# Attention with a routed feed-forward on one core: flag and index loads, part of the early second layer, the gate of the weight loads and the fill of the plain arms moved

## The chip, the core and the metric

The kernel runs on one core of a Trainium2 chip. A core has TensorE (PE in the profile; its weight loads are the row PEld), VectorE (DVE), ScalarE (ACT), GpSimd (POOL) and SyncE (SP), each with an instruction stream of its own; they meet through semaphores, and data moves through 16 DMA engines. The metric is the device time of one execution in microseconds.

## The reference, cut to what matters

Chunked attention (4 batches, 8 heads, 768 positions of 64 numbers) gives 3072 tokens of 512 numbers. Each token then goes through the one expert out of eight that scores highest for it.

```python
for c in range(nc):                                    # chunks of 32 queries
    k_full = np.concatenate([mem_k, k_ctx], axis=2)    # 8 memory keys, 16 left, own 32, 8 right
    scores = scale * np.matmul(q_c, k_full.transpose(0, 1, 3, 2))
    a = softmax(scores)
    out[:, :, c_start:c_end] = np.matmul(a, v_full)
x = out.transpose(0, 2, 1, 3).reshape(B * S, H * D)
logits = x @ w_gate                                    # [3072, 8]
expert_idx = np.argmax(logits, axis=1)
for e in range(E):                                     # the tokens of expert e
    h = np.maximum(x_sorted[lo:hi] @ w1[e], 0.0)       # 512 -> 1024
    y_sorted[lo:hi] = h @ w2[e]                        # 1024 -> 512
y = gate_w[:, None] * y_sorted[inv_perm]
```

How many tokens an expert gets is known only at run time. Everything is float32, and a float32 matmul shows as two records of PE and two of PEld.

## The kernel before, in words

**Attention stage (to about 140 us of the span).** 32 blocks of 96 tokens go through transposes, scores, exponentials and values. Behind them run the logits, the routing and a scatter of each block's rows to `x_dram`, ordered by expert (`scatter_one`, on POOL). The scatters wait in the list `spread`, and `scatter_some` issues them; each is made to follow the last PE instruction that was issued before it (`behind`).

**Early rows.** The first 256 rows of expert 0 are computed while the routing of the last blocks is still under way. `early_ops` is a list of closures: one transposition, eight pieces of the first layer (`first`), then the second layer of the first 128 rows in four parts (`part_of`). Each part holds 4 float32 matmuls of 256 columns; the second and the fourth end with `early_out`, an ACT operation that writes half of the row block `y00`.

**End of the stage.** `count_up` is a chain of some forty small DVE operations that makes the tables of the experts' stage: `cases` (which arm each expert takes, and a flag that says whether it is a plain one), `bases` (first rows), `rows`, `good`. Then engines read such values into registers: PE reads the arm's number of every expert (`load_index`, L1228), DVE and ACT read six flags each (`plain_on`, L1243), and all read `good` (L1244). Between them PE does the last early parts. `nc.tensor.addr_align(PAGE, 0, 0)` makes PE go on at the start of a page of 256 instructions.

**Barrier.** `tc.tile_critical` (L1821, L1899) opens the experts' stage. All engines wait there for what was issued before. SP waits for the last scatter to land and for ACT's last operation (L1821) and then lets the others go (L1899).

**Experts' stage.** Its plan is written out by hand: `op` notes an instruction with the semaphore counts that it needs, `emit` issues it. On PE each expert has an interlude and a `Switch`, a jump table with one arm for each width and form:

* An interlude transposes the results of the expert before (`turn_y`, L538). That of expert 0 instead does the second layer of the early rows 128 to 255 (tile `sum_z`, 8 float32 matmuls of 512 columns).
* A **split** arm multiplies the two halves of the tokens by a seven-product scheme: 14 products for the first layer, 7 for the second, 448 LDWEIGHTS and MATMUL instructions in all.
* A **plain** arm, for experts 1 to 6 with at most 240 tokens, multiplies directly (`plain`). Four `pair` calls make the first layer (banks P, Q, Z, P) and two the second. The last bank is filled in two column halves (`groups=2`), which gives twice as many matmuls of half the width: 80 float32 matmuls, 320 instructions, so the arm reaches into a second page.
* Near its end an arm issues a hint for the arm of the next expert (L1813); the branch out of the arm and the jump of the next `Switch` have line L1829.

In this execution expert 1 (200 tokens wide, from 211.4 us) and expert 6 (168, from 420.3 us) take plain arms. The others take split ones.

**Counts in a plain arm.** Other engines wait for PE's and ACT's running counts, and both forms of an arm must end on the same ones. A split arm adds 21 to PE's count, one for each product. A plain arm sets the counts by `upto`: in `before` the four pairs of the first layer bring PE to 1, 2, 3 and 14 of 21, the rest to 15, 16, 17, 18 and 21. ACT's seven outputs bring its count to 1 to 6 and then, with the last one, to the end.

**SP's queue.** For each expert SP issues, in this order, the rows of the next one (`load_x`, 8 DMAs, L1417), w1 of the one after it (`get_w(e + 2, 0)`, 4 DMAs of 512 KB, L1490) and its w2 (`get_w(e + 2, 1)`, one DMA of 2 MB, L1489). The weights of expert e + 2 replace those of e, so each load waits until PE and DVE have read the old ones.

On DVE and ACT an `If` on the flag of the expert chooses between the instructions of the two forms (L1845).

Of the kernel before, what the change touches and what calls it, by code (L numbers as in the profile page):

```python
# [82 lines left out]
PAGE = 256  # L83
LB = 16
# [442 lines left out]
def ordinary(ctx, tc, q, k, v, mem_k, mem_v, moe_w_gate, moe_w1, moe_w2, out, good):  # L527

    nc = tc.nc
# [542 lines left out]
    def early_rows():  # L1072

        x0T = e0pool.tile([128, DM // 128, NER], F32, name="x0T")
        def turn_early():
            nc.vector.transpose(
                x0T.rearrange("p k (b j) -> p k b j", j=32), x0.rearrange("p b (k i) -> p k b i", k=4)
            )

        def first(f):  # L1080
            ph = ps_s.tile([128, 2, 512], F32, tag="s", name="ph0")[:, 0, 0:NER]
            for c in range(DM // 128):
                mm(
                    ph,
                    lhsT=ms[0]["w1"][:, c, 128 * f : 128 * f + 128],
                    rhs=x0T[:, c],
                    start=c == 0,
                    stop=c == DM // 128 - 1,
                )
            nc.scalar.activation(h0[:, f], ph, AF.Relu)  # L1090

        hold = {}

        def part_of(part):
            half, f = part // 2, F // 256 * (part % 2)
            if part % 2 == 0:
                hold["y"] = ps_s.tile([128, 2, 512], F32, tag="s", name="py0")
            py, sl = hold["y"][:, 0, 0 : DM // 2], slice(DM // 2 * half, DM // 2 * half + DM // 2)
            second_layer(py, 0, range(f, f + F // 256), sl)
            if part % 2 == 1:  # L1100
                early_out(0, py, sl)

        early_ops.append(turn_early)
        for f in range(F // 128):
            early_ops.append(lambda f=f: first(f))
        for part in range(4):
            early_ops.append(lambda part=part: part_of(part))
# [5 lines left out]
    with tc.manual_schedule():  # L1113
# [112 lines left out]
        def load_index(*of):  # L1226
            for e in of:
                index.append(nc.tensor.value_load(cases[0:1, e : e + 1], min_val=0, max_val=len(arms_of(e)) - 1))  # L1228

        while spread:  # L1230
            if len(early_ops) == 3:
                load_index(0, 1, 2)
            do_early(1)
            scatter_some(1)
# [3 lines left out]
        assert len(index) == 3 and len(early_ops) == 2  # L1238
        plain_on = {}
        for name, eng in (("DVE", nc.vector), ("ACT", nc.scalar)):  # L1240
            for e in range(E):
                if can_be_plain(e):
                    plain_on[name, e] = eng.value_load(cases[0:1, E + e : E + e + 1], min_val=0, max_val=1)  # L1243
# [3 lines left out]
        load_index(3, 4)  # L1247
        do_early(1)
        load_index(5, 6, 7)
# [36 lines left out]
    def op(eng, fn, reads=(), writes=(), dma=None, where="after", pace=False, by=16, upto=None):  # L1286
# [6 lines left out]

        if pace:
            after(("PE", counts["PE"]))
# [187 lines left out]
    def get_w(e, which):  # L1483
# [8 lines left out]
        op("SP", fn, [], [(name, e % 2, q) for q in ("21", "rest")], dma=f"{name}{e % 2}", by=(64, 16)[which])  # L1492
# [145 lines left out]

    def interlude(e):

        before = ("before", e)
        if e == 0:
# [8 lines left out]
            for i in range(3):  # L1651
                sums1[0][0][i]()
            for part in range(4):
                op("PE", lambda n, part=part: second_layer(Z[:, 0], 1, [2 * part, 2 * part + 1]), [], ["z0"], where=before)
# [13 lines left out]
    def plain(e, ends):  # L1668
# [36 lines left out]
        mid = start["PE"] + 14  # L1705
        for j, (bank, names) in enumerate((sums_p, sums_q, sums_z, sums_p)):
# [7 lines left out]
                mid if j == 3 else start["PE"] + j + 1,  # L1714
# [8 lines left out]
        for m, (bank, names) in enumerate((sums_q, sums_p)):  # L1723
# [7 lines left out]
            if m == 0:  # L1731
                first = [("h", a, b, 0) for a in range(2) for b in range(2) if a * b == 0]
                pair(*second, w2n + first, mid + 1, of=range(C2 - 2))
                pair(*second, [("h", 1, 1, 0)], mid + 2, of=range(C2 - 2, C2))
# [11 lines left out]
    def expert(e):  # L1746
# [14 lines left out]
        def usual():  # L1761
# [10 lines left out]
            assert not sends  # L1772
            if e < E - 1:
                get_x(e + 1)
                tick()
# [26 lines left out]
    for g in range(2):  # L1802
        sends.append(lambda pace, g=g: op("POOL", one_op(lambda: put(early["y", g], lab0[:, g, 0:1])), [("yb", NY - 1)] if g else [], [], dma=f"early{g}", pace=True))
# [17 lines left out]
    with tc.tile_critical(no_gpsimd_drain=True):  # L1821
# [14 lines left out]
        for name in ("POOL", "SP", "ACT", "DVE"):  # L1836
            eng, done = engines[name], set()
            for s in (s for s in plan if s[0] == name):
                if s[4] == "after":
                    emit(s)  # L1840
                elif s[4][1] not in done:
                    e = s[4][1]
                    done.add(e)
                    if (name, e) in plain_on:
                        with eng.If(plain_on[name, e]):  # L1845
                            for x in steps(name, ("plain", e)):
                                emit(x)
# [56 lines left out]
```

## Time and profile before

| what | us |
|---|---|
| runs of this kernel, median of 3 (lowest, highest) | 503.57 (502.87, 503.97) |
| the profiled execution | 503.97 |
| its span, first to last instruction | 502.2 |
| PE busy | 472.9 |
| PEld busy | 440.1 |
| DVE busy | 282.0 |
| ACT busy | 207.4 |
| POOL busy | 145.9 |

The profiled execution is the slowest of the three runs. Its span leaves out 1.8 us around the first and the last instruction. PE is the engine that is busy nearly all the time, so the places to look at are those where it stands still or runs slowly. In a timeline, the bracket behind an instruction is the idle time of its engine before it, and what ended it; "issue" means that the engine waited for nothing that the profile shows, its sequencer for example.

### The profile page before, as it was taken

To read this page: it belongs to the slowest core of one execution; us is meant where nothing else is said; L and a number is where in the kernel's file an instruction comes from. 1 tells how busy PE (TensorE), PEld (TensorE's weight loads), DVE (VectorE), ACT (ScalarE), POOL (GpSimd) and SP (SyncE) were. 2 spreads that over 40 slices of the span, in tenths; PEclk is the share of its full clock that TensorE was granted. 3 is DMA by queue.
4 is the path that set the end of the run, shared out by engine and by line. 5 is a ranking of instruction groups with operands and counts; after the bars stand their busy time and mean duration, and the time that the engine had idled before them with its cause. 6 is when DMAs were issued, how large, how long until landed. Compare 5 with 4: busy or idle time off the path is not lost. (4 is left out here: it accounts for less than half of the span.)

```text
span 502.2 us, 9216 instructions
## 1 busy us (share of the span) xinstructions
PE 472.9 (94%) x3320; PEld 440.1 (88%) x3320; DVE 282.0 (56%) x548; ACT 207.4 (41%) x388; POOL 145.9 (29%) x191
## 2 busy tenths in 40 slices
PE   4999999999999699997799999999999999999993
PEld 3899999999997479997799999987778999989992
DVE  4466587667556178922446666655346776445511
ACT  3676666566621046311253155243313643144312
POOL 3000223313434127334034134313230550352003
PEclk9999999999999899999699999999999999999997
DMA  9999998899898289789805294583432986500002
GB/s 220 182 208 208 228 263 228 223 217 280 232 233 263 71 253 196 189 249 209 239 31 123 50 281 128 109 230 105 99 72 65 301 171 194 136 6 27 1 0 87
DMA packets 103059, 82.99 MB, mean 165 GB/s; under 512 B 40309, under 2 KB 85966, under 8 KB 102992
## 3 DMA queue, kind: packets, MB, share of 16 engines
q1 hardware_dynamic: 94576, 67.94, 57.6%
q0 software_dynamic: 6912, 13.54, 8.1%
q8 instruction: 45, 0.74, 0.7%
q10 hardware_dynamic: 1504, 0.59, 0.5%
q14 instruction: 22, 0.18, 0.1%
HBM read 65.62 MB, written 21.28 MB: 173 GB/s over the span
## 5 line engine op out<-in xcount | busy, mean ns | idle before, releaser
L1452 POOL DMA_INDIRECT out_dram<-y,lab x42 | 48.7, 1159 | 155.4 <-ACT y L1439 30.9
L934 POOL DMA_INDIRECT lab<-x_dram,rows x42 | 52.8, 1258 | 53.1 <-PE sum_r L533 19.8
L533 PE MATMUL sum_p<-xsT,w 128*128 128x144 f32 (+7 forms) x256 | 50.8, 345 | 4.9 <-issue 3.8
L533 PE MATMUL o<-v,ex 128*96 128x65 f32 x512 | 52.8, 246 | 0.0
L533 PEld LDWEIGHTS o<-v,ex 128*96 128x96 f32 x512 | 50.4, 165 | 1.4 <-issue 1.3
L533 PEld LDWEIGHTS sum_p<-xsT,w 128*128 128x128 f32 x256 | 42.8, 194 | 9.7 <-issue 5.7
L533 PE MATMUL sum_p<-h,w 128*128 128x144 f32 (+9 forms) x320 | 50.4, 314 | 0.0
L533 PE MATMUL sc<-qT,kT 128*128 128x192 f32 x256 | 49.2, 336 | 0.0
L533 PEld LDWEIGHTS sum_p<-h,w 128*128 128x128 f32 x320 | 46.3, 191 | 2.4
L847 POOL DMA_INDIRECT x_dram<-xr,dest x32 | 29.6, 926 | 54.9 <-PE o L533 36.0
L704 ACT ACTIVATE ex<-sc,cst 128x256 f32<-128x256 f32 x96 | 38.5, 471 | 13.8 <-PE sc L533 11.6
L1388 ACT COPY sum_r<-sum_p 128x640 f32<-128x640 f32 x36 | 24.4, 677 | 46.0 <-PE sum_p L533 45.7
L533 PEld LDWEIGHTS sc<-qT,kT 128*128 128x128 f32 x256 | 42.0, 195 | 0.0
L655 ACT COPY qT<-tqk 64x384 f32<-64x384 f32 x60 | 30.0, 500 | 28.6 <-PE tqk L538 27.8
L673 DVE COPY kT<-tqk 64x384 f32<-64x384 f32 x58 | 32.0, 552 | 11.0 <-PE tqk L538 10.2
L533 PE MATMUL sum_q<-t,s 128*128 128x144 f32 (+5 forms) x192 | 38.2, 348 | 0.0
L533 PE MATMUL sum_r<-t,w 128*128 128x144 f32 (+5 forms) x192 | 37.0, 340 | 0.0
L533 PE MATMUL sum_p<-t,s 128*128 128x144 f32 (+5 forms) x192 | 37.0, 341 | 0.0
L533 PEld LDWEIGHTS sum_q<-t,s 128*128 128x128 f32 x192 | 33.2, 196 | 2.5
L533 PEld LDWEIGHTS sum_p<-t,s 128*128 128x128 f32 x192 | 32.2, 191 | 2.4
L1406 DVE STREAM_TRANSPOSE xsT<-xs 128x1280 f32<-128x1280 f32 (+1 forms) x16 | 22.4, 1427 | 20.6 <-DMA xs<-x_dram 11.3
L533 PEld LDWEIGHTS sum_r<-t,w 128*128 128x128 f32 x192 | 31.8, 190 | 2.3
(183 smaller groups left out, 774.8 us busy)
## 6 DMA issues: line engine op xcount, KB each, us to landing
w<-in_moe_w_dram SPq DMA_DIRECT2D x36, 512.0 KB
w<-in_moe_w_dram SPq DMA_DIRECT2D x7, 2048.0 KB, 11.5
xs<-x_dram SPq DMA_DIRECT2D x56, 160.0 KB
kn<-in_k_dram SPq DMA_DIRECT2D x16, 384.0 KB
qn<-in_q_dram SPq DMA_DIRECT2D x16, 384.0 KB
x_dram<-zeros SPq DMA_DIRECT2D x8, 396.0 KB
v<-in_v_dram SPq DMA_DIRECT2D x24, 128.0 KB
v<-in_v_dram SPq DMA_DIRECT2D x24, 112.0 KB
```

Of the source, the lines that this page charges most:

```text
L533: i = nc.tensor.matmul(*args, **more)
L655: copy(to[:, :, :, t], tq[D * t : D * t + D])
L673: i = copy(to, of[:, :, 0:PAIRS].rearrange("d a (y z p) -> d a y z p", y=2, z=2))
L704: nc.scalar.activation(ex4[:, :, :, sl], sc4[:, :, :, sl], AF.Exp, bias=mask[:, 3 * x + g : 3 * x + g + 1], scale=D**-0.5)
L847: i = nc.gpsimd.indirect_dma_start(out=x_dram, out_offset=bass.IndirectOffsetOnAxis(ap=dest[:, t : t + 1], axis=0), in_=xr[:, t % NXR].bit ...
L934: return nc.gpsimd.indirect_dma_start(out=to.bitcast(I32), out_offset=None, in_=x_dram.rearrange("r (k c) -> (r k) c", c=LB), in_offset=ba ...
L1388: op("ACT", one_op(lambda: nc.scalar.copy(to, of)), reads, writes)
L1406: op("DVE", one_op(lambda: nc.vector.transpose(to, of)), [("xs", y, a) for a in range(4)], [("x", k, 1 - y) for k in range(2)])
L1452: return nc.gpsimd.indirect_dma_start(out=out, out_offset=bass.IndirectOffsetOnAxis(ap=which.bitcast(I32), axis=0), in_=y, in_offset=None, ...
```

## The change

* **Early second layer.** Of the row block `y00`, columns 0 to 255 are computed as before in two parts. Columns 256 to 383 (`EARLY_COLUMNS`) are one part of 8 matmuls of 128 columns. Columns 384 to 511, 8 more of 128 columns, go behind the barrier to the head of expert 0's interlude, into the second bank of `Z`, with an `early_out` of their own on ACT.
* **Order at the end of the stage.** In the last loop a scatter is issued ahead of the early part and no longer behind it.
* **Index loads.** PE reads one arm number ahead of the barrier. The other seven are read between the four parts of expert 0's interlude (`with_index`).
* **Flags.** DVE and ACT read the flag of expert e + 1 right behind the instructions of expert e, in the experts' stage. None is read ahead of the barrier.
* **Weight loads.** w1 of expert e + 2 also waits for ACT's count after the first layer of expert e in the split form, w2 for ACT's count at the end of expert e. In a plain arm ACT's count reaches both with its last output only.
* **Plain arms.** The last bank is filled without column halves, which leaves 64 float32 matmuls of full width. Ahead of each, PE gets two waits (for counts of ACT and DVE that it has already seen at the start of the arm). PE's count now rises in ninths of the whole (`share`).

```diff
         early_ops.append(turn_early)
         for f in range(F // 128):
             early_ops.append(lambda f=f: first(f))
-        for part in range(4):
-            early_ops.append(lambda part=part: part_of(part))
+        early_ops.append(lambda: part_of(range(F // 256), slice(0, DM // 2)))
+        early_ops.append(lambda: part_of(range(F // 256, F // 128), slice(0, DM // 2)))
+        early_ops.append(lambda: part_of(range(F // 128), slice(DM // 2, EARLY_COLUMNS)))
...
         while spread:
-            if len(early_ops) == 3:
-                load_index(0, 1, 2)
+            scatter_some(1)
+            if len(early_ops) == 2:
+                load_index(0)
             do_early(1)
-            scatter_some(1)
...
-        plain_on = {}
-        for name, eng in (("DVE", nc.vector), ("ACT", nc.scalar)):
-            for e in range(E):
-                if can_be_plain(e):
-                    plain_on[name, e] = eng.value_load(cases[0:1, E + e : E + e + 1], min_val=0, max_val=1)
         rv = nc.values_load(good[0:1, 0:1], min_val=0, max_val=1)
         tc.switch_hint({mybir.EngineType.PE: index[0]}, len(arms_of(0)), "expert0")
         nc.tensor.addr_align(PAGE, 0, 0)
-        load_index(3, 4)
-        do_early(1)
-        load_index(5, 6, 7)
         do_early(1)
...
+    def with_index(part, made):
+
+        for e in range(2 * part + 1, min(2 * part + 3, E)):
+            load_index(e)
+        return made
...
+            rest_of = slice(EARLY_COLUMNS, DM)
+            last = Z[:, 1, 0 : DM - EARLY_COLUMNS]
+            op("PE", lambda n: second_layer(last, 0, range(F // 128), rest_of), [], ["z1"], where=before)
+            op("ACT", one_op(lambda: early_out(0, last, rest_of)), [], ["z1", "y00"])
             for part in range(4):
-                op("PE", lambda n, part=part: second_layer(Z[:, 0], 1, [2 * part, 2 * part + 1]), [], ["z0"], where=before)
+                op("PE", lambda n, part=part: with_index(part, second_layer(Z[:, 0], 1, [2 * part, 2 * part + 1])), [], ["z0"], where=before)
...
                         for c in of or range(chunks):
+                            for x in ("ACT", "DVE"):
+                                nc.tensor.wait_ge(sems[x], passed[x])
                             made.append(
...
-        mid = start["PE"] + 14
+        all_of, passed = ends["PE"] - start["PE"], dict(known["PE"])
+
+        def share(k):
+
+            return start["PE"] + all_of * k // 9
...
-                pair(*second, [], mid + 3, halves=[0], groups=2)
+                pair(*second, [], share(7), halves=[0])
                 out(yT[:, 2, 1], ("y", 1, 0), P[:, 0], ["p0"], AF.Copy, start["ACT"] + 6)
-                pair(*second, [], mid + 4, halves=[1], groups=2, at=[0])
-                pair(*second, [], ends["PE"], halves=[1], groups=2, at=[1])
+                pair(*second, [], share(8), halves=[1], of=range(C2 // 2))
+                pair(*second, [], ends["PE"], halves=[1], of=range(C2 // 2, C2))
...
             assert not sends
+            half.append(("ACT", counts["ACT"]))
...
+        half = []
         either(e, usual, (lambda ends: plain(e, ends)) if can_be_plain(e) else None)
         if e + 2 < E:
-            get_w(e + 2, 0)
+            get_w(e + 2, 0, half)
...
-            get_w(e + 2, 1)
+            get_w(e + 2, 1, [("ACT", counts["ACT"])])
...
+                    if name in ARMED and e + 1 < E and can_be_plain(e + 1):
+                        plain_on[e + 1] = eng.value_load(cases[0:1, E + e + 1 : E + e + 2], min_val=0, max_val=1)
```

More of the change, by code (lines that the diff above doesn't have):

```diff
@@ L83 @@
 PAGE = 256
+EARLY_COLUMNS = 384
 LB = 16
@@ L1092, in early_rows, with part_of @@
         hold = {}
-        def part_of(part):
-            half, f = part // 2, F // 256 * (part % 2)
-            if part % 2 == 0:
+        def part_of(fs, sl):
+            if fs[0] == 0:
                 hold["y"] = ps_s.tile([128, 2, 512], F32, tag="s", name="py0")
-            py, sl = hold["y"][:, 0, 0 : DM // 2], slice(DM // 2 * half, DM // 2 * half + DM // 2)
-            second_layer(py, 0, range(f, f + F // 256), sl)
-            if part % 2 == 1:
+            py = hold["y"][:, 0, 0 : sl.stop - sl.start]
+            second_layer(py, 0, fs, sl)
+            if fs[-1] == F // 128 - 1:
                 early_out(0, py, sl)
@@ L1224, in ordinary, with load_index @@
         index = []
-        def load_index(*of):
-            for e in of:
-                index.append(nc.tensor.value_load(cases[0:1, e : e + 1], min_val=0, max_val=len(arms_of(e)) - 1))
+        def load_index(e):
+            index.append(nc.tensor.value_load(cases[0:1, e : e + 1], min_val=0, max_val=len(arms_of(e)) - 1))
         while spread:
-            if len(early_ops) == 3:
-                load_index(0, 1, 2)
+            scatter_some(1)
+            if len(early_ops) == 2:
+                load_index(0)
             do_early(1)
-            scatter_some(1)
         zeroed = end_rows(0)
@@ L1237, in ordinary @@
             tc.declare_no_dep(zeroed.ins, j, reason="rows behind those of the tokens")
-        assert len(index) == 3 and len(early_ops) == 2
-        plain_on = {}
-        for name, eng in (("DVE", nc.vector), ("ACT", nc.scalar)):
-            for e in range(E):
-                if can_be_plain(e):
-                    plain_on[name, e] = eng.value_load(cases[0:1, E + e : E + e + 1], min_val=0, max_val=1)
+        assert len(early_ops) == len(index) == 1
         rv = nc.values_load(good[0:1, 0:1], min_val=0, max_val=1)
@@ L1284, in ordinary, with op @@
     ARMED = ("PE", "ACT", "DVE")
-    def op(eng, fn, reads=(), writes=(), dma=None, where="after", pace=False, by=16, upto=None):
+    def op(eng, fn, reads=(), writes=(), dma=None, where="after", pace=False, by=16, upto=None, also=()):
         need = {}
@@ L1292, in after @@
                 need[sem] = max(need.get(sem, 0), n)
+        for stamp in also:
+            after(stamp)
         if pace:
@@ L1481, in batch, with get_w @@
             plan.append((eng, one_op(fn), need, (sem, 16), "after"))
-    def get_w(e, which):
+    def get_w(e, which, also=()):
         name = ("w1", "w2")[which]
@@ L1490, in fn @@
             return [nc.sync.dma_start(w[32 * a : 32 * a + 32], w1_rows(e, a)) for a in range(4)]
-        op("SP", fn, [], [(name, e % 2, q) for q in ("21", "rest")], dma=f"{name}{e % 2}", by=(64, 16)[which])
+        op("SP", fn, [], [(name, e % 2, q) for q in ("21", "rest")], dma=f"{name}{e % 2}", by=(64, 16)[which], also=also)
     def quarters(e, layer):
@@ L1713, in plain @@
                 [("w1", e % 2, "rest"), ("w1", e % 2, "21")] + [("x", k, 0) for k in range(2)],
-                mid if j == 3 else start["PE"] + j + 1,
+                share(j + 1),
             )
@@ L1802, in ordinary @@
     for g in range(2):
-        sends.append(lambda pace, g=g: op("POOL", one_op(lambda: put(early["y", g], lab0[:, g, 0:1])), [("yb", NY - 1)] if g else [], [], dma=f"early{g}", pace=True))
+        sends.append(lambda pace, g=g: op("POOL", one_op(lambda: put(early["y", g], lab0[:, g, 0:1])), [("yb", NY - 1)] if g else ["y00"], [], dma=f"early{g}", pace=True))
     for e in range(E):
@@ L1836, in ordinary @@
         for name in ("POOL", "SP", "ACT", "DVE"):
-            eng, done = engines[name], set()
+            eng, done, plain_on = engines[name], set(), {}
             for s in (s for s in plan if s[0] == name):
@@ L1843, in ordinary @@
                     done.add(e)
-                    if (name, e) in plain_on:
-                        with eng.If(plain_on[name, e]):
+                    if e in plain_on:
+                        with eng.If(plain_on[e]):
                             for x in steps(name, ("plain", e)):
```

4 lines of the change are left out of this document (2 added, 2 removed).

## Prediction

> **What bounds the kernel now.** I read the page first, then PE's timeline over the experts' stage, then what PE's sequencer and SP did where PE stood still.
>
> ```profile
> span 502.2 us, 9216 instructions
> PE 472.9 (94%) x3320; PEld 440.1 (88%) x3320; DVE 282.0 (56%) x548; ACT 207.4 (41%) x388; POOL 145.9 (29%) x191
> ```
>
> PE is the bound. What can be won are its gaps, its slow stretches and matmuls it need not do. The timeline of PE, around the ends of the two plain arms (expert 1 above, expert 6 below):
>
> ```profile
> 222.36 5.58 PE L533 MATMUL sum_q<-h,w 128*128 128x200 f32 x32
> 227.77 7.29 PE L533 MATMUL sum_p<-h,w 128*128 128x96 f32 x64
> 237.60 1.12 PE L538 MATMUL sum_z<-cst,yT 128*128 128x128 f32 x4 [2.54 <-issue]
> ...
> 244.48 3.24 PE L533 MATMUL sum_p<-xsT,w 128*128 128x216 f32 x8 [3.11 <-issue]
> ...
> 252.00 1.62 PE L533 MATMUL sum_r<-xsT,w 128*128 128x216 f32 x8
> 253.46 1.62 PE L533 MATMUL sum_p<-xsT,w 128*128 128x216 f32 x8
> ...
> 429.46 4.72 PE L533 MATMUL sum_q<-h,w 128*128 128x168 f32 x32
> 434.02 7.27 PE L533 MATMUL sum_p<-h,w 128*128 128x80 f32 x64
> 441.14 0.60 PE L538 MATMUL sum_z<-cst,yT 128*128 128x128 f32 x4
> 441.57 1.04 PE L538 MATMUL sum_q<-cst,yT 128*128 128x128 f32 x8
> ...
> 443.97 1.93 PE L533 MATMUL sum_p<-xsT,w 128*128 128x248 f32 x8 [0.48 <-issue]
> ```
>
> The same code runs twice. Behind expert 6, PE goes from the arm to the next expert's first product in 443.97 - 441.14 = 2.83 us. Behind expert 1 it waits 2.54 us and again 3.11 us for "issue", and afterwards its products are slow: three take 252.00 - 244.48 = 7.52 us where the next takes 1.46. The views of line L1829 (the branches, on PE's sequencer) in the two windows, the loads that SP issues, the queue's bytes from 228.0 to 234.5 us, and the granted clock from 245 to 250 us say why:
>
> ```profile
> L1829 PEldq COMPARE_BRANCH  x2: 4176/4410/4643, 232.9 to 240.1; - x2
> L1829 PEldq COMPARE_BRANCH  x2: 381/434/487, 439.1 to 443.3; - x2
> 225.59 1.75 SPq L1490 DMA_DIRECT2D w<-in_moe_w_dram  x4
> 235.09 0.38 SPq L1489 DMA_DIRECT2D w<-in_moe_w_dram  x1
> q1 hardware_dynamic: 388, 1.39, 103.9%
> 245.00:250.00 5.00, 5.00 (x15) 4.71 (x14) 1.27 (x2) 0.68 (x1) 0.00 (x0) 0.50 0.80 161
> ```
>
> Two branches of 4.64 and 4.18 us there, 0.38 and 0.49 us here. I read them as waits for the page of code that the branch goes to: behind expert 1 this page must come through DMA engines that the loads of w1 and w2 of expert 3 keep full (103.9%), and expert 6 has no such loads. Behind the gaps the clock is at 0.50. The Trainium skill agrees on the mechanism ("Runtime: NRT & Kernel Launch", section "Instruction fetch mechanics": code comes in blocks of 256 instructions, and a taken branch out of the loaded window waits for its block).
>
> The second place is the barrier: timelines of PE, POOL, ACT and DVE, SP's waits, and the register loads.
>
> ```profile
> 158.60 1.89 PE L533 MATMUL py<-w,h 128*128 128x256 f32 x8
> 161.21 1.99 PE L533 MATMUL py<-w,h 128*128 128x256 f32 x8 [0.72 <-issue]
> 165.17 5.40 PE L533 MATMUL py<-w,h 128*128 128x256 f32 x16 [1.97 <-issue]
> 172.38 0.45 PE L533 MATMUL sum_r<-nought 128*128 128x320 bf16 x2 [1.80 <-issue]
> 172.66 7.03 PE L533 MATMUL sum_z<-w,h 128*128 128x512 f32 x16
> 180.48 1.25 PE L533 MATMUL sum_p<-xsT,w 128*128 128x144 f32 x8 [0.80 <-DVE xsT L1406]
> 160.77 0.92 POOL L847 DMA_INDIRECT x_dram<-xr,dest  x1 [0.30 <-issue]
> 163.48 0.91 POOL L847 DMA_INDIRECT x_dram<-xr,dest  x1 [1.79 <-PE py L533]
> 170.61 0.47 ACT L1070 ACTIVATE y<-py,lab 128x256 f32<-128x256 f32 x1 [6.85 <-PE py L533]
> 162.48 0.18 DVE L1024 TENSOR_SCALAR rows<-far 128x40 int32<-128x40 f32 x1
> SPq L1821 <- DMA x_dram<-xr,dest: 4.4, 1, 4.4
> SPq L1821 <- ACT y L1070: 3.8, 1, 3.8
> L1228 PEldq TENSOR_LOAD <-cases x8: 299/305/804, 158.6 to 166.8; - x8
> L1244 PEldq TENSOR_LOAD <-good x1: 1347/1347/1347, 161.3 to 161.3; - x1
> L1243 ACTq TENSOR_LOAD <-cases x6: 277/286/707, 163.3 to 167.0; - x6
> ```
>
> SP waits first for the last scatter, then 3.8 us for ACT's `early_out`, which ends at 171.08, and that one for PE's last early part. PE loses 0.72 us to three loads and 1.97 us to `good`, the page change and two more loads. Its last 16 records take 5.40 us, where 16 at the pace of the first row (1.73 for 8) take 3.5. Behind the barrier expert 0 starts at 180.48, when DVE has turned its rows; PE itself is free at 172.66 + 16 x 0.428 = 179.5.
>
> **The change part by part.**
>
> *Column halves.* Expert 1: 64 records to the arm's end (227.77 to about 234.9, by the same group's 441.14 - 434.02 = 7.12 in expert 6) become 32 at the pace of the bank before, (227.77 - 222.36)/32 = 0.169, so 5.41: **-1.7**. Expert 6: 7.12 against 32 x (434.02 - 429.46)/32 = 4.56: **-2.6**.
>
> *Padding waits.* 128 waits per arm. The trace has PE's barrier waits (line L1899, window of 167.4 to 167.95):
>
> ```profile
> L1899 PEldq EVENT_SEMAPHORE  x5: 51/51/3314, 167.5 to 167.9; - x5
> ```
>
> Five in 0.4 us, 0.1 each, and there each holds two conditions. Ahead of a matmul of two records (0.285 to 0.339 us of array) stand 0.1 us, or 0.2 if the two stay apart. The conditions are met long before, and the sequencer runs ahead of the array, so I take 0; the other end is a sequencer-bound arm, where the whole gain of the halves is lost (+4.3). The instructions stay as many: 16 matmuls x 4 fewer, 64 double waits more, so the page boundary stays near and the second page is still reached.
>
> *Weight loads.* In expert 1's arm w1 and w2 of expert 3 now leave only after ACT's last output, about 0.4 us after PE's end, some 8 us later than 225.59 by the arm's own clock. The pages that PE needs next (the arm's exit, the next expert's arm) are hinted within the arm, the last one 4 matmuls before its end, while the sequencer runs ahead of the array (it reaches the exit branch at 232.9, 2 us before the array's end). So I take them to come through free engines, as behind expert 6. The other end is that nothing of the 6.8 and 3.1 below is won. So 244.48 - 234.9 = 9.6 becomes 2.83, **-6.8**, and without long gaps the clock stays up: 7.52 becomes 3 x 1.46, **-3.1**. Behind SP's waiting loads stand only rows for expert 3. In split arms w1 and w2 leave one ACT output (0.7 us) later; the rows of expert 7 too:
>
> ```profile
> 431.48 1.51 DVE L1406 STREAM_TRANSPOSE xsT<-xs 128x1280 f32<-128x1280 f32 x1 [9.08 <-issue]
> 437.75 0.82 DVE L1385 TENSOR_TENSOR t<-xsT 128x640 f32<-128x640 f32 x1
> ```
>
> That chain ends at 438.6 + 0.7, its first reader (the second product of expert 7) is due at 443.97 - 2.6 + 1.7 = 443.1. Nothing.
>
> *Counts in ninths.* POOL's stores and label gathers in a plain arm are paced by PE's count, and so are spread over it where they came in bursts. w1's old condition (14 of 21) is met later in the arm, but ACT's comes last anyway. The stores are read by nobody, the labels at the end of the next expert, some 40 us on. DVE's transpositions of the next rows wait for the end of the first layer as before. 0.
>
> *Ahead of the barrier.* One index load instead of three: part two follows part one without a gap, from 160.3 to 162.1. `good` is loaded during it, from 160.1; at its 1.35 us, with the 1 us of hint and page change behind it, PE's last part starts at about 162.5. It is now 16 records of 128 columns at (441.57 - 441.14)/4 = 0.108, 1.7 us, and ACT's output of 128 columns takes some 0.4: 164.8 instead of 171.08, **-6.3**. The ends: 161.5 (load of 0.3) to 164.4 at half clock. What is late next: the scatter, moved one PE step ahead, leaves at 160.77 instead of 163.48 and so lands at 164.4; DVE ends at 162.66 and has one load instead of seven; ACT has shed six. All before 164.8, but close.
>
> *Behind the barrier.* PE gets 16 records more, 1.7 us: free at 181.2 instead of 179.5 on the old clock, past DVE's 180.48: **+0.75**. Seven index loads: each 0.3 plus about as much of register work, two per part, beside parts of 4 x 0.428 = 1.7 us. Hidden; at 1.35 us each they would cost about 4. `early_out` of the late columns falls into ACT's idle time. The flags: one load of 0.3 to 0.7 us per expert on DVE and ACT, beside their last operation of an arm (0.8 and 0.7): 0.
>
> **Sum.** -6.3 + 0.75 - 1.7 - 6.8 - 3.1 - 2.6 = -19.75. From the profiled execution, 503.97: 484.2. It is 0.4 above the median, 503.57, so the forecast is **483.8**.
>
> **Rivals.**
>
> *The stall behind expert 1 stays* (493.7). The page would then be late because it is asked for late, whatever the engines do, and the end of expert 1's arm would look as before. The Trainium skill speaks for it: "DMA: Bandwidth & Descriptors", section "Queues, rings and completion order", has each DMA engine switch between queues after every packet, so that a page should wait for one packet at most. By that rule no weight load could hold a page for microseconds. Against it: 0.38 us for the same branch of the same code without loads. Price 6.8 + 3.1. 8%.
>
> *The barrier gains half.* If PE's last part again finds a gap of 2 us and runs at half clock (the row of 165.17 did), it starts at 164.1, takes 3.5 and the barrier is at 168.4: 487.4. 10%.
>
> *The waits bind the plain arms*, the change's halves give nothing: 488.1. 4%.
>
> *Slower.* One mechanism: w1, w2 and the rows for expert 3 now start at 233.8 instead of 225.6 on the clock of expert 1. Over 225 to 260 us they were
>
> ```profile
> q1 hardware_dynamic: 4304, 5.51, 64.0%
> 276.64 2.90 DVE L1406 STREAM_TRANSPOSE xsT<-xs 128x1280 f32<-128x1280 f32 x2
> ```
>
> 5.51 MB, and DVE needs the rows at 276.6 - 11.6 = 265. It decides from under 5.51 MB/31 us = 177 GB/s; to eat the whole gain they must land at 285, at 108 GB/s. The engines moved 1.39 MB in 6.5 us, 214 GB/s. 2%, at about 505.
>
> *Nothing changes*, since gains of this kind are taken back by a wait that I do not see: 2%.
>
> **How the numbers follow.** The forecast's own case (483.8, from 481.5 with a quick load of `good` and no gap behind expert 1, to 486) has 74%. The range takes in the barrier's and the waits' rivals and a stall that stays in part: 481 to 490. A measurement of this kernel tells about 0.2% (1 us) from no change. Faster 0.96, same 0.02, slower 0.02.
>
> **What would show it.** In the profile after: branches L1829 behind expert 1 under 0.6 us and no "issue" gap over 1 us there; the loads of line L1490 starting behind ACT's last output of the arm; clock 1.00 in the first products of expert 2; the last bank of a plain arm as 32 records of 200 and 168 columns; ACT's `early_out` ahead of the barrier ending 6 us earlier; expert 0's first product released by PE itself and no longer by DVE. Wrong would be a 4 us branch with no load beside it, a wait of DVE for the rows of expert 3, or plain matmuls spaced wider than 0.17 us.

## The result, and the profile after

The median goes from 503.63 us (502.87 to 503.97) to 489.06 (488.05 to 490.83): a ratio of 0.9717, 95% interval 0.9684 to 0.9749. The profiled execution took 488.05 us, its span 486.2. A second series of the same kernel gave 0.9716 (0.9675 to 0.9758). Each ratio is to the kernel before in the same series, whose median was 502.52 to 504.08 us. Two executions are left out of all comparisons because they ran slow as a whole: one of 1244.53 us of the barrier's part alone, and one of 494.29 us, the one that was profiled, in the second series of the kernel after.

PE's timeline of the kernel after, first around the barrier, then from expert 0's end over expert 1's arm, then behind expert 6's arm (start, duration, line, output and inputs, shape, count; in brackets the idle time before and what ended it):

```profile
158.28 5.75 PE L534 MATMUL py<-w,h 128*128 128x256 f32 x32
166.09 0.45 PE L534 MATMUL sum_r<-nought 128*128 128x320 bf16 x2 [2.06 <-issue]
166.37 8.82 PE L534 MATMUL sum_z<-w,h 128*128 128x128 f32 x32
175.02 1.14 PE L534 MATMUL sum_p<-xsT,w 128*128 128x144 f32 x8
...
203.16 0.60 PE L539 MATMUL sum_z<-cst,yT 128*128 128x128 f32 x4
...
207.43 2.95 PE L534 MATMUL sum_p<-xsT,w 128*128 128x200 f32 x16 [1.73 <-DVE t L1379]
...
223.74 5.58 PE L534 MATMUL sum_p<-h,w 128*128 128x200 f32 x32
229.16 0.60 PE L539 MATMUL sum_z<-cst,yT 128*128 128x128 f32 x4
...
232.11 1.72 PE L534 MATMUL sum_p<-xsT,w 128*128 128x216 f32 x8 [0.34 <-issue]
233.66 1.62 PE L534 MATMUL sum_q<-t,s 128*128 128x216 f32 x8
...
418.85 4.72 PE L534 MATMUL sum_p<-h,w 128*128 128x168 f32 x32
425.53 0.65 PE L539 MATMUL sum_z<-cst,yT 128*128 128x128 f32 x4 [1.96 <-DVE t L1379]
...
428.00 1.30 PE L534 MATMUL sum_p<-xsT,w 128*128 128x248 f32 x5
```

Ahead of the barrier the second layer now runs without a gap. Expert 0 is no longer released by DVE. The stall behind expert 1 is gone, and expert 2's first products start 1.55 us apart, at full pace. Two waits are new: 1.73 us ahead of expert 1 and 1.96 us behind expert 6's arm, both put down to the same line of DVE. Only the second is DVE's. Ahead of expert 1 the releaser that the timeline names had long been done, and PE's sequencer was held, as the branches show (line L1842 in two windows; minimum, median and maximum in ns, from when to when):

```profile
L1842 PEldq COMPARE_BRANCH  x2: 474/1024/1574, 201.0 to 205.6; - x2
L1842 PEldq COMPARE_BRANCH  x2: 312/364/415, 226.1 to 231.6; - x2
```

Behind expert 1 both branches fell under 0.42 us (4.64 and 4.18 before). Ahead of expert 1 one rose from 0.47 to 1.57. The same stretches between starts in PE's timeline, before and after, with what the prediction gave them:

```
from .. to                                        before   after   change   predicted
early rows' second layer .. expert 0's product     21.88   16.74    -5.14       -5.55
expert 0's transpositions .. expert 1's product     2.70    4.27    +1.57        0
expert 1's product .. expert 2's product           33.05   24.68    -8.37       -8.5
expert 2's product .. its transpositions           44.02   40.97    -3.05       -3.1
expert 6's product .. expert 7's product           23.72   22.91    -0.81       -2.6
```

The rest moves by less than 0.4 us in sum. (Experts 3, 4 and 5 take as long from their first product to their transpositions as before, within 0.02 us.) So the sum of 19.75 lost 1.6 and 1.8 us in two places and 0.4 at the barrier: 15.9 between the two profiled executions.

### The profile page after: what moved, and what is told of

The parts are those of the page before. It is cut to its first block, busy times and chain, and to the rows that moved or that the text cites. A ratio compares the mean times of both kernels' runs of the same rounds, so it can differ in the third digit from the quotient of the medians.

```text
span 486.2 us, 9257 instructions
## 1 busy us (share of the span) xinstructions
PE 462.1 (95%) x3272; PEld 431.4 (89%) x3272; DVE 282.5 (58%) x548; ACT 207.8 (43%) x389; POOL 146.1 (30%) x191
## 5 line engine op out<-in xcount | busy, mean ns | idle before, releaser
L1446 POOL DMA_INDIRECT out_dram<-y,lab x42 | 50.3, 1198 | 149.0 <-ACT y L1433 30.8
L935 POOL DMA_INDIRECT lab<-x_dram,rows x42 | 51.3, 1222 | 53.9 <-PE sum_q L534 19.6
L534 PE MATMUL sum_p<-xsT,w 128*128 128x144 f32 (+7 forms) x256 | 49.1, 337 | 2.7 <-DVE t L1379 1.7
L534 PEld LDWEIGHTS sum_p<-xsT,w 128*128 128x128 f32 x256 | 41.8, 190 | 7.0 <-issue 2.6
L534 PE MATMUL sum_p<-h,w 128*128 128x144 f32 (+7 forms) x256 | 46.1, 335 | 0.0
L534 PEld LDWEIGHTS sum_p<-h,w 128*128 128x128 f32 x256 | 41.8, 190 | 2.4
L534 PE MATMUL sum_q<-t,s 128*128 128x144 f32 (+5 forms) x192 | 36.7, 339 | 0.0
L534 PEld LDWEIGHTS sum_q<-t,s 128*128 128x128 f32 x192 | 31.9, 190 | 2.3
```

The costliest lines, as they stand in the source:

```text
L534: i = nc.tensor.matmul(*args, **more)
L935: return nc.gpsimd.indirect_dma_start(out=to.bitcast(I32), out_offset=None, in_=x_dram.rearrange("r (k c) -> (r k) c", c=LB), in_offset=ba ...
L1446: return nc.gpsimd.indirect_dma_start(out=out, out_offset=bass.IndirectOffsetOnAxis(ap=which.bitcast(I32), axis=0), in_=y, in_offset=None, ...
```

## The experiments

**The three parts alone.** Each is the kernel before with one part of the diff. First the gate:

```diff
-            get_w(e + 2, 0)
+            get_w(e + 2, 0, half)
...
-            get_w(e + 2, 1)
+            get_w(e + 2, 1, [("ACT", counts["ACT"])])
```

> The kernel before with one part of the change: both weight loads of an expert wait for ACT (w1 for ACT's output of the first layer, w2 for its last). Theory 1 (the page of code behind expert 1 is late because the loads of w1 and w2 fill the DMA engines while it is asked for): both branches behind expert 1 fall under 0.6 us, the clock stays at 1.00 in the first products of expert 2, and 6.8 + 3.1 = 9.9 us go. Theory 2 (the page is asked for late, whatever the loads do): the branches stay at 4 us, 503.6 us within 1. A second question goes with it: the kernel after has a new branch of 1.57 us ahead of expert 1's arm (0.47 before). If the gate makes it, because w1 of expert 2 leaves later in expert 0 and is still under way when PE asks for that page, it shows here too, and the time is 503.6 - 9.9 + 1.6 = 495.3 us; if the earlier barrier makes it, it does not show, and the time is 493.7 us.

495.40 us, ratio 0.9841 (0.9805 to 0.9878), which is 8.0 us. Its branches ahead of expert 1 and behind it:

```profile
L1833 PEldq COMPARE_BRANCH  x2: 497/947/1397, 205.1 to 209.4; - x2
L1833 PEldq COMPARE_BRANCH  x2: 399/410/422, 232.4 to 236.9; - x2
```

Both halves of the expectation came in: the stall goes, and the gate itself makes the late branch ahead of expert 1 (1.40 us), with the old barrier in place.

The barrier's part alone (columns cut at 384, index loads and flags behind the barrier):

> The kernel before with the barrier's part alone: second layer of the early rows cut at 384 columns, index loads and flags behind the barrier. Expert 0's first product moved by 180.48 - 175.02 = 5.46 us in the kernel after. Theory 1 (the parts add, and the late page ahead of expert 1's arm comes from the gate): 503.6 - 5.5 = 498.1 us, that branch near 0.5 us, the stall behind expert 1 as before (branches over 4 us). Theory 2 (the earlier barrier makes that page late, since the loads of expert 2 do not move with it): branch of 1.6 us, 499.7 us. Theory 3 (the gain is given back in waits for the loads that start no earlier): 503 us.

Ratio 0.9942 (0.9908 to 0.9975): 2.9 us (1.3 to 4.6), about half of the 5.5. The branch ahead of expert 1 stayed under 0.5 us, so theory 2 is out; the stall behind it stayed too. The missing half lies at the barrier itself: in this profile expert 0 starts 19.76 us behind the start of the second layer, where it was 16.74 in the profile after. This is taken up below.

The plain arms' part alone (no column halves, the padding waits, ninths):

> The kernel before with the plain arms' part alone: no column halves, the padding waits, counts in ninths; weight loads wait for PE's count as before. Theory 1 (the halves are worth 1.7 us in expert 1 and 2.6 us in expert 6, the waits nothing): last bank 32 records at 0.17 us (expert 1) and 0.14 us (expert 6); behind expert 6 DVE's chain of transpositions and sums ends as the arm does (438.6 against 441.14 - 2.56 = 438.6), so that almost all of the 2.6 is kept; 503.6 - 4.3 = 499.3 us. Theory 2 (the stall behind expert 1 ends when the loads do, so what expert 1 wins is lost in it): 501.0 us. Theory 3 (the sequencer binds the arms with 128 more waits): 503.6 us, records spaced wider than 0.17 us.

497.51 us, ratio 0.9875 (0.9839 to 0.9911): 6.3 us, more than any theory gave. Its branches behind expert 1:

```profile
L1836 PEldq COMPARE_BRANCH  x2: 417/2489/4561, 229.8 to 234.8; - x2
```

The DMA queues there, from 226 to 227.5 us and from 227.5 to 236 (packets, MB, share of 16 engines):

```profile
q8 instruction: 1, 0.02, 4.7%
...
q1 hardware_dynamic: 451, 1.65, 87.6%
q0 software_dynamic: 14, 0.01, 0.5%
```

One of the two stalls behind expert 1 is gone without the gate. A page of code (queue q8) came in just ahead of the load of w1, which leaves at 227.58, and none during it; the second branch, which had no page, took 4.56 us. So the padding waits do more than fill: they bring the request of the exit's page ahead of the load. In the kernel before, the load had been under way since 225.59 when that request fell due (with the gate alone, whose arm is the same, the page comes between 228 and 231 us):

```profile
q1 hardware_dynamic: 3326, 3.36, 79.8%
q0 software_dynamic: 400, 0.56, 8.9%
...
q1 hardware_dynamic: 70, 0.29, 95.7%
q8 instruction: 1, 0.02, 5.7%
```

These are its queues from 216 to 234.5 us, where no page came in, and from 234.5 to 236.

The three parts alone make 8.0 + 2.9 + 6.3 = 17.2 us. The first stall, 2.7 us (26.17 - 23.46 between expert 1's product and its transpositions, before and with the gate), is in two of them; without it 14.5 remain, and the whole change has 503.6 x 0.0283 = 14.3. Each of the three has an interval of 1.7 to 1.9 us to either side, so the agreement is rough.

**What the padding waits cost.** The kernel after without them:

```diff
-                            for x in ("ACT", "DVE"):
-                                nc.tensor.wait_ge(sems[x], passed[x])
```

> The kernel after without the padding waits of the plain arms (they wait for nothing that is not met already). Theory 1 (the waits cost nothing; what they do is to bring PE's sequencer into the arm's second page of code early, where the page of the arm's exit is asked for: 15.7 us behind the arm's first product in the profile after, some 3 us later in the kernel before's arms): without them that page is asked for at the exit alone, where a page that is not there took 3.7 us at the end of the kernel after with no load beside it; the sequencer is 3.0 us ahead of the array there, so each plain arm loses some 0.7 to 1.5 us behind it: 490.5 to 492 us. Theory 2 (the sequencer binds the arms through the waits): the plain arms get shorter than 21.7 and 18.3 us, 485 to 488 us. Theory 3 (neither): 489.1 us within 0.5.

493.12 us, ratio 0.9816 (0.9789 to 0.9843): slower, by 4 to 5 us than the kernel after and by some 3 us than two kernels of its own series below (0.9748 and 0.9754), and 1 us above the upper of theory 1's numbers. PE's timeline behind expert 1:

```profile
226.00 5.58 PE L534 MATMUL sum_p<-h,w 128*128 128x200 f32 x32
231.72 0.65 PE L539 MATMUL sum_z<-cst,yT 128*128 128x128 f32 x4
...
235.18 1.72 PE L534 MATMUL sum_p<-xsT,w 128*128 128x216 f32 x8 [1.05 <-issue]
```

Its branches behind experts 1 and 6:

```profile
L1840 PEldq COMPARE_BRANCH  x2: 1121/2200/3278, 228.4 to 233.9; - x2
...
L1840 PEldq COMPARE_BRANCH  x2: 401/1988/3575, 423.9 to 430.6; - x2
```

The last bank takes 5.58 us with the waits and without: they cost nothing. Without them both exits' branches take 3.28 and 3.58 us, with no weight load beside them. The queues say when the page came, in the kernel after from 222 to 225 us and here from 229 to 231:

```profile
q8 instruction: 1, 0.02, 1.9%
```

```profile
q0 software_dynamic: 25, 0.01, 4.7%
q8 instruction: 1, 0.02, 2.9%
```

In the kernel after it comes at least 1 us ahead of the exit's branch (226.1), here behind it (228.4). The Trainium skill ("Runtime: NRT & Kernel Launch", section "Instruction fetch mechanics") has the sequencer fetch the next page while it executes the current one, and the trace fits: the arm now has more instructions ahead of its end, so PE enters the arm's second page sooner (this follows from the count; no record shows it directly). The profile shows only 0.8 us of the loss, behind expert 1 (25.51 us from product to product where after has 24.68). Of the 4.3 us between the two spans, 2.7 lie ahead of expert 0 and 1.1 behind the last expert's transpositions, where profiles of other kernels differ as much. The rest of the loss in the times stays open.

**The wait behind expert 6.** The kernel after, DVE's order changed in the plain arms:

```diff
-        turn_x(e + 1, 0)
-        turn_x(e + 1, 1)
         s1, t1 = sums1[e + 1]
         for f in (s1[0], s1[1]):
             f()
+        turn_x(e + 1, 0)
+        turn_x(e + 1, 1)
```

> The kernel after, with one thing moved in the plain arms: DVE takes the two weight sums of the next expert ahead of the transpositions of its rows, instead of behind them. Theory 1 (behind expert 6 PE waits 1.96 us for DVE, because its count is reached only with the last operation of a chain that starts when the rows land: two transpositions, two weight sums, one token sum; the weight sums do not need the rows): the chain behind the landing loses 1.18 + 1.23 = 2.4 us, PE's wait ahead of the transpositions goes, 489.1 - 2.0 = 487.1 us. Theory 2 (PE's wait is for the rows themselves or for DVE's outputs, or what is won there is lost at the next product): the wait stays or moves, 489.1 us within 0.5.

DVE's timeline behind the landing of expert 7's rows, first of the kernel after, then of this one, and PE's of this one:

```profile
418.63 1.51 DVE L1400 STREAM_TRANSPOSE xsT<-xs 128x1280 f32<-128x1280 f32 x1 [11.54 <-DMA xs<-x_dram]
420.81 1.51 DVE L1400 STREAM_TRANSPOSE xsT<-xs 128x1280 f32<-128x1280 f32 x1 [0.67 <-DMA xs<-x_dram]
422.24 1.18 DVE L1379 TENSOR_TENSOR s<-w 128x1024 f32<-128x1024 f32 x1
423.46 1.23 DVE L1379 TENSOR_TENSOR s<-s,w 128x1024 f32<-128x1024 f32 x1
424.60 0.87 DVE L1379 TENSOR_TENSOR t<-xsT 128x640 f32<-128x640 f32 x1
```

```profile
425.45 1.51 DVE L1400 STREAM_TRANSPOSE xsT<-xs 128x1280 f32<-128x1280 f32 x1 [0.63 <-DMA xs<-x_dram]
427.07 0.82 DVE L1379 TENSOR_TENSOR t<-xsT 128x640 f32<-128x640 f32 x1
```

```profile
423.68 4.72 PE L534 MATMUL sum_p<-h,w 128*128 128x168 f32 x32
428.24 0.60 PE L539 MATMUL sum_z<-cst,yT 128*128 128x128 f32 x4
```

In the kernel after, PE's transpositions start at 425.53, when DVE's last operation of the chain ends (424.60 + 0.87 = 425.47). They read nothing of that chain; they wait for a count of DVE that the plain arm reaches only with its last operation. With the sums first PE goes on at once, and expert 6 takes 21.06 us from product to product: the 2.6 us of the column halves are all there. Theory 1 holds in the profile. The time does not show it: 490.66 us (487.71 to 492.08), ratio 0.9726 (0.9684 to 0.9767). In the profiled execution, the one of 492.08 us, the second layer of the early rows starts 2.2 us later than in that of after, the barrier takes 19.70 us (16.74 in after), and the way from the last expert's transpositions to the end 0.9 us more. How it was in the other executions is not shown.

**The load of w1 in expert 0, and the order of the last scatter.**

```diff
-            get_w(e + 2, 0, half)
+            get_w(e + 2, 0, half if can_be_plain(e) else [])
```

> The kernel after, but the load of w1 for expert 2 (issued in expert 0) waits for PE's count alone, as before the change. In the profile after it leaves 16.4 us behind expert 0's first product (before: 14.6 us) and PE's branch into expert 1's arm takes 1.57 us (before: 0.47). Theory 1 (the load is still under way when PE asks for the pages of code, and holds them): the branch falls to 0.5 us, the way from expert 0's transpositions to expert 1's first product from 4.27 to 2.7 to 3.0 us; 489.1 - 1.4 = 487.7 us. Theory 2 (the pages are late because two are asked for at once, and the load has nothing to do with it): the branch stays above 1.1 us, 489.1 us within 0.5.

The branch takes 0.81 us instead of 1.57, and expert 1 starts 3.51 us behind expert 0's transpositions. The three later runs with this edit had 3.11, 3.18 and 3.10. Six profiles with the gate there have 3.63 to 4.27 (mean 3.86), seven without it 2.70 to 3.51 (mean 3.10): the gate costs 0.8 us at this place, half of the 1.57 that the profile after shows. The time, 490.30 us (ratio 0.9748, 0.9724 to 0.9772), cannot tell it.

Then the last scatter, issued with the one ahead of it:

```diff
-            scatter_some(1)
+            scatter_some(2 if len(early_ops) == 3 else 1)
```

> The kernel after, with the last scatter of token rows issued one PE step earlier, together with the one ahead of it. In the profile after the last scatter leaves at 160.45, 0.8 us ahead of the zeros behind expert 0's rows, and lands 2.9 us later; in the profile of the run with the sums first, whose barrier is the same code, it leaves at 163.02, 0.2 us behind the zeros, and lands 5.0 us later, the barrier opens 3.4 us behind ACT's output, and expert 0 starts 19.7 us behind the start of the second layer of the early rows instead of 16.7. Theory 1 (the order of the scatter and the zeros on the DMA engines decides): the scatter now always leaves first, 16.7 us or less, and a median of 489.1 - 1.5 = 487.6 us with a smaller spread. Theory 2 (what is late is the attention stage itself or the zeros): 19 to 20 us can still come, median 489.1 us within 0.7.

491.11 us (488.04 to 492.29), ratio 0.9754 (0.9724 to 0.9784): theory 1 is out. Theory 2 comes nearer, though the time that it gave lies 2 us lower, and in this profile the barrier took 17.40 us. The scatter now lands in time, and SP waits for the zeros instead. What SP waits for at the barrier (total, times, longest, us), in the kernel after, in the one with the sums first, and here:

```profile
SPq L1834 <- DMA x_dram<-zeros: 1.3, 1, 1.3
SPq L1834 <- DMA x_dram<-xr,dest: 0.6, 1, 0.6
```

```profile
SPq L1834 <- DMA x_dram<-xr,dest: 3.5, 1, 3.5
```

```profile
SPq L1838 <- DMA x_dram<-zeros: 1.9, 1, 1.9
```

ACT's output has ended in all three, in the kernel after at 164.43, while SP's wait for the zeros ends at 164.8:

```profile
164.06 0.37 ACT L1071 ACTIVATE y<-py,lab 128x128 f32<-128x128 f32 x1 [1.41 <-PE py L534]
```

(With the sums first, 1.3 us lie between ACT's output and the end of SP's wait for the scatter. The 3.4 us of the expectation are close to PE's idle time there, 3.34. And the order of scatter and zeros does not decide alone: in the profile of the barrier's part alone the scatter left at 162.35, 0.9 us ahead of the zeros, and SP still waited for it until 167.7.) So the barrier of the change opens with the landing of a DMA. Its length, from the start of the second layer to expert 0's product, is 16.74, 17.40, 18.39, 19.39, 19.61, 19.70 and 19.76 us in seven profiles (mean 18.7), where three with the barrier of before have 20.60 to 21.88 (mean 21.3). The profile after is the shortest of its kind. The mean gain of 2.6 us agrees with the 2.9 (1.3 to 4.6) of the barrier's part alone. The barrier is not the only stretch that varies: in thirteen profiles the second layer of the early rows starts at 157.68 to 160.84 us, and from the last expert's transpositions to the end it is 12.88 to 14.37.

A part of the spread is the clock. PE's share and the granted clock just behind the barrier, in the kernel after and in the one with the sums first (window, length, busy time and records of the five engines, clock, DMA share, GB/s):

```profile
166.40:170.00 3.60, 3.60 (x22) 2.64 (x22) 3.38 (x3) 1.31 (x3) 0.99 (x2) 1.00 0.65 168
```

```profile
169.90:173.00 3.10, 3.10 (x18) 2.86 (x18) 3.03 (x3) 0.63 (x2) 0.97 (x2) 0.65 0.55 136
```

The 32 records that stand there, 16 of them put there by the change, take 8.82 us at clock 1.00 and 10.48 behind the longer gap (3.34 us). Of the seven profiles, two have 8.82 and five 10.06 to 10.48.

**All three moves, and the columns back ahead of the barrier.** First the sums, w1 and the scatters together:

> The kernel after with three moves together: the weight sums ahead of the transpositions in the plain arms (2.1 us of expert 6's arm in a profile), the load of w1 for expert 2 by PE's count alone, the last two scatters together. Theory 1 (each removes a wait that the profile after shows, and they stand in different places, so they add): 489.1 - 2.1 - 1.4 - 1.5 = 484.1 us, between 483 and 486. Theory 2 (what is won in one place is lost at the next wait): above 487 us.

487.59 us (486.15 to 487.82), ratio 0.9689 (0.9665 to 0.9713), 1.6 us above the upper of theory 1's numbers and where theory 2 had it. Two of the three gains are there in the profile all the same (expert 6 gives 21.12 us, the way to expert 1 3.11). The third is not: the barrier took 19.39.

If a DMA opens the barrier, the second layer's columns need not stand behind it. The kernel after with `EARLY_COLUMNS = 512` and without the rest behind the barrier:

> The kernel after with all 512 columns of the early rows' second layer ahead of the barrier again (16 records of 256 columns as part three instead of 128), everything else as after. PE then ends 1.75 us later ahead of the barrier and starts expert 0's work behind it 1.75 us lighter. Theory 1 (the barrier now opens with a DMA's landing, 6.6 to 7.9 us behind the start of that second layer, not with ACT's output at 6.2, so the columns ahead of it cost next to nothing; behind it DVE's rows are the next bound, 8.0 us, where PE took 8.9 to 10.6): 0.5 to 1.5 us faster than after in the same runs. Theory 2 (ACT's output releases the barrier, as the prediction had it): 1.75 us later ahead of it and 0.75 won behind it, 1.0 us slower than after.

PE's timeline at its barrier:

```profile
160.84 7.42 PE L534 MATMUL py<-w,h 128*128 128x256 f32 x32
170.03 0.45 PE L534 MATMUL sum_r<-nought 128*128 128x320 bf16 x2 [1.76 <-issue]
170.31 7.03 PE L534 MATMUL sum_z<-w,h 128*128 128x512 f32 x16
177.69 1.25 PE L534 MATMUL sum_p<-xsT,w 128*128 128x144 f32 x8 [0.35 <-DVE xsT L1400]
```

The barrier takes 16.85 us, 16.86 and 16.57 in the two runs below. PE's gap shrinks to 1.76 us, and `sum_z` takes 7.03 us, as before the change. 489.22 us, ratio 0.9702 (0.9669 to 0.9736), beside 0.9716 (0.9675 to 0.9758) for the kernel after in the same series: the intervals overlap, and the time alone excludes neither theory. What opens this barrier is ACT's output again, as theory 2 had it. Its row here, and SP's wait in the first of the two runs with 512 columns below:

```profile
168.30 0.47 ACT L1071 ACTIVATE y<-py,lab 128x256 f32<-128x256 f32 x1 [3.28 <-PE py L534]
```

```profile
SPq L1834 <- ACT y L1071: 2.6, 1, 2.6
```

PE goes on 170.03 - 168.77 = 1.26 us behind this output, and 1.2 to 1.3 in the two runs below. In the kernel before, where ACT released it, it was 172.38 - 171.08 = 1.30; in the seven profiles with 384 columns it is 1.65 to 3.05. On the price theory 1 is right: SP's wait for the scatter had ended 0.3 us earlier, so the columns ahead of the barrier lengthen it by next to nothing.

One more thing moved in this profile. Expert 6 takes 21.33 us from product to product, 1.6 less than in after, with DVE's order as it was: SP issued the rows of expert 7 in 9.67 us where it took 11.24, and PE waited 0.29 us instead of 1.96. So the wait behind expert 6 also differs between executions.

The kernel after in that series:

> The kernel after once more, beside the next three on the same chip. The profile after may have met a good barrier: from the start of the early rows' second layer to expert 0's first product it took 16.75 us, where six other profiles with the barrier of the change took 17.4 to 19.8 and three with the barrier of before 20.6 to 21.9. Theory 1 (where the zeros and the last scatter land decides, and it differs from execution to execution): 17 to 20 us, a median near 490 us. Theory 2 (the barrier of the change takes 16.75 us, and the other kernels' differ because of what was changed in them): 16.75 within 0.3.

486.54 to 491.49 us, median 490.88, near the 490 of theory 1. This series adds no barrier to the list; that the shortest one was one of many rests on the seven profiles above. Then the moves with 512 columns, with and without the scatters together:

> The kernel with the three moves (sums first, w1 of expert 2 by PE's count, last two scatters together; 487.6 us) and all 512 columns ahead of the barrier. Theory 1: 487.6 - 1.0 = 486.6 us, within 0.7. Theory 2 (ACT's output releases): 488.6 us.

> As the run before, but with the last scatter where the change put it: sums first, w1 of expert 2 by PE's count, 512 columns ahead of the barrier. With the scatters together the zeros landed last in two profiles, without it the scatter or the zeros, at about the same time. Theory 1 (the order of the two does not matter, whichever comes last holds the barrier for the same time): within 0.7 us of the run with four moves. Theory 2 (the scatters together are worth something): 1.5 us slower than it.

487.51 us, ratio 0.9683 (0.9647 to 0.9719), and 486.92, ratio 0.9671 (0.9638 to 0.9703). No difference shows, as theory 1 had it, and the barriers agree (16.86 and 16.57); the times alone are too coarse to exclude the 1.5 us of theory 2. The last (sums first, w1 of expert 2 by PE's count, all columns ahead of the barrier) has the lowest ratio of all, 0.9671 beside 0.9716 for the kernel after in the same series, or 2.3 us; these intervals overlap too.

## Why the prediction was right, and where it was not

It said 483.8 us, from 481 to 490; it is 489.06. The sign and the main terms held, and the forecast was 5.3 us too low. The time lies outside the forecast's own case (481.5 to 486 us, 74%) and 1 us inside the range, whose upper end had been set for rivals that did not come as they were named. That three losses which it had put at nothing still fit into it is in part luck.

- **The stall behind expert 1 (-6.8) and the slow clock (-3.1): right.** With the halves of expert 1 (-1.7) the stretch gave 8.37 of 8.5 us, the clock 3.05 of 3.1, and the gate alone shows both. The reading needs one correction. A branch of 4 us was read as a page that full DMA engines hold up. But an exit without its page takes 3.28 to 3.58 us with free engines, and such a branch beside the loads took 4.18 to 4.96 in three profiles (before, and the barrier's and the plain arms' parts alone), so the load adds 0.6 to 1.7 to that. What the load does is to keep away the page that was asked for early, and that early request is the reason for the 0.38 us behind expert 6. Whether the request waits or is lost under the load, the runs do not tell. The Trainium skill's rule that was a rival ("DMA: Bandwidth & Descriptors", section "Queues, rings and completion order") fits the small addition. It does not explain that the page asked for early had not come by 234.5 us, where a page then came within 1.5 us beside a queue at 95.7%.
- **Costed at nothing: the gate in expert 0.** "In split arms w1 and w2 leave one ACT output (0.7 us) later" was right for w2 and short for w1, which left 1.9 us later behind expert 0's start, and what was missed is that PE asks for pages there too. It costs 0.8 us in the mean, 1.6 in the profile after.
- **Column halves of expert 6 (-2.6): half right.** The bank is as forecast (4.72 us for 32 records). The step that failed is "That chain ends at 438.6 + 0.7, its first reader (the second product of expert 7) is due at 443.97 - 2.6 + 1.7 = 443.1. Nothing." Its first waiter was PE's transposition of expert 6's own output, by way of DVE's count, due 2.56 us earlier than before. In the kernel before, the chain had ended 441.14 - 438.57 = 2.57 us ahead of that transposition: the halves used up this slack, and rows that landed later took the rest. 1.8 us were lost between the two profiles; in the run with 512 columns and DVE's order as it was, where the rows came sooner, it was 0.2.
- **Padding waits (0): right in price, their use not seen.** Without them the arms are no shorter, and their exits get slower.
- **Barrier (-6.3, then +0.75): right in the profile shown, not in the mean.** ACT's output ended at 164.43 (forecast 164.8, though its terms, 162.5 + 1.7 + 0.4, make 164.6) and expert 0 moved by 5.46 us (5.55) in the profile's own time. The step that failed is "All before 164.8, but close": the scatter's landing was put at 164.4 from one row, and the zeros behind expert 0's rows were not priced at all. One of them lands last in all seven profiles, 0.4 to 1.5 us behind ACT's output (1.1 in the mean). And the slow clock of five of them, at a gap of PE of 2.06 us in one and 3.05 or more in four, which the forecast left out, lengthens the 32 records behind the barrier by 1.2 to 1.7 us (1.1 in the mean of the seven). The rival of half the gain was right in size (2.6 to 2.9 us), by another cause than the one it named.
- **Flags, index loads, ninths (0): right.** The experts' arms and the ways between them are within 0.15 us of before wherever no wait named above stands.
- **The slower rival did not come**: expert 3 starts 2.57 us behind expert 2's transpositions, 2.54 before.

The means: barrier 18.7 us instead of 21.88 - 5.55 = 16.3, so 2.4 less; expert 6, 1.8 less; the gate in expert 0, 0.8. That is 5.0 of the 5.3 us, closer than such means can be trusted: the profiles are of several kernels, and the attention stage and the end alone differ by 3.2 and 1.5 us between them.

## What to carry to other kernels

When a term shortens a stretch, look for everything that ran beside it with little to spare, and ask who waits for it through a count, not only who reads its data. A barrier has as many ends as it waits for: price each landing from more than one execution before its gain is counted. And where the program branches, place the request for the next code ahead of the loads; the instructions of an arm, even waits that are met, decide when that is.

## What was not expected of the hardware

A page of code that is asked for at the branch costs 3.3 to 3.6 us on an otherwise quiet chip, not much less than beside the weight loads (4.2 to 5.0). And the length of PE's gap alone did not tell the clock behind it: the kernel after and the one without padding waits both stood 2.06 us ahead of the barrier's work, and the same 32 records then took 8.82 us in one and 10.47 in the other, where the granted clock was 0.59 at first:

```profile
167.10 0.45 PE L534 MATMUL sum_r<-nought 128*128 128x320 bf16 x2 [2.06 <-issue]
167.38 10.47 PE L534 MATMUL sum_z<-w,h 128*128 128x128 f32 x32
```

```profile
167.40:171.00 3.60, 3.60 (x19) 3.10 (x18) 3.44 (x3) 1.04 (x2) 0.99 (x2) 0.59 0.61 159
```

A gap of 2.70 us (scatters together) cost no clock; the four of 3.05 to 3.46 us did.
